# A head pair's sums moved ahead of the last score tile, its transfers moved to SyncE, and PSUM copies given precedence in the second stage

## The chip, the core and the metric

The kernel runs on one core of one Trainium2 chip. The metric is device microseconds of one execution; a median of three runs is given, and one further execution was taken with the hardware profiler. Engines are named as in the profile: PE is TensorE (PEld its weight loads), DVE is VectorE, ACT is ScalarE, POOL is GpSimd, SP is SyncE, which only issues transfers here.

## What is computed

Soft-capped attention over 4 batches of 12 heads (448 tokens, 64 dimensions each), whose output, as 1792 rows of 768, goes through a two-layer block with a rational activation:

```python
scores = cap * np.tanh(scale * np.matmul(q, k.transpose(0, 1, 3, 2)) / cap)
attn = np.exp(scores - np.max(scores, axis=-1, keepdims=True))
attn = attn / (np.sum(attn, axis=-1, keepdims=True) + 1e-09)
x = np.matmul(attn, v)            # then heads side by side: 1792 x 768
h = x @ w_in                      # 768 x 2048
P = a[0] + a[1] * h + a[2] * h2 + a[3] * h3
Q = 1.0 + np.abs(b[0]) * np.abs(h) + np.abs(b[1]) * h2
out = (P / (Q + 1e-6)) @ w_out    # 2048 x 768
```

Every product is carried at nearly full float32 precision by splitting both factors in a high and a low part and adding three products. `w_in` and `w_out` arrive as 8-byte floats and are rebuilt on the chip as 4-byte ones.

## The kernel before, in words

**Attention** walks over 24 pairs of heads, `p` = 0 to 23. Each pair has up to four score tiles (`scores`, L412: `n` = 0, 1, 2, and on odd pairs a tile 3 that holds the last 64 keys of both pairs). ACT takes the hyperbolic tangent in place in PSUM (`softmax`, L424) and the exponential into SBUF (`exp`, L442); DVE adds the exponentials of a pair's tiles up (L448, tiles `es`). `pv` (L496) multiplies with the values, `pv_tails` (L513) adds the last 64 keys. Score tiles rotate over three two-bank PSUM tiles (`ps_127`, `ps_128`, `ps_129` in the listings, `PS[0]` to `PS[2]`); the PV products use the banks `pv` and `mi`.

`norm(k)` handles the two pairs 2k and 2k+1 together. `sums` (L541) lets PE add the exponentials over keys, into `mi`, for the very last `k` into `PS[2]`. DVE copies the result out (L545). Four small transfers gather it into a compact tile (`sc`, in the listings `arena_f<-arena_f`); DVE adds a guard and takes the reciprocal (L554, L555); one transfer writes that to DRAM (`dn<-arena_f`) and two broadcast it back (`arena_r<-dn`). Each waits for the one ahead. The last `norm` has these seven transfers on SP's queue, all others on POOL's. `xout` (L574) then multiplies each pair's PV output with it, and `split_x` makes the high part on ACT (L585) and the low part on DVE (L586).

**The second stage** walks over 8 groups `g` of 256 hidden columns, two halves `m` of the tokens, and two 128-column units `y`: 32 units. `stage1` (L778) is 36 matmuls into one PSUM tile. `rational` (L809 to L822) is a chain of ACT steps (absolute value, square, linear term, logarithm L814, exponential L816, cast L821) and DVE steps (L813, L815, L817, L818, L819, L820, L822). `stage2` (L847) multiplies with `w_out`: for each pair of units 7 tiles of 128 tokens, 12 matmuls each, alternately in `PS[1]` and in the banks `pv` and `mi`. The result is copied out of PSUM: for `m` = 0 by ACT into one of three buffers (L874), from which it is written or added to `out`; for `m` = 1 into accumulators, in the first group by ACT (L877), later by DVE (L880). `make_w` rebuilds a weight tile (ACT L725, DVE L727, L730, L733) and splits it (ACT L755, DVE L757); its load (`load_w`, 768 KB, on SP) needs the one raw buffer that the steps before have read.

**What sets the order.** Every step is recorded by `self.op` with a cost, its reads and its writes, and `Plan.flush` orders them engine by engine, on modelled times: of the steps that are ready about when an engine comes free it takes the one with the lowest `prio`, which is the place in the program minus `early`. In the chip each engine and each queue then works strictly in that order. The place in the program during attention is set by `visits(p)`, a list written by hand for each pair:

```python
            return [s0, s1, (pv, p - 1), s2, t, *new, (norm, p // 2 - 1)]
```

So on an odd pair `p` the sums of the pairs `p - 3` and `p - 2` come after all four score tiles; on the last pair, 23, these are the sums of pairs 20 and 21, `norm(10)`. The sums of pairs 22 and 23, `norm(11)`, follow after attention.

Of the kernel before, what the change touches and what calls it, by code (L numbers as in the profile page):

```python
# [16 lines left out]
ALU = mybir.AluOpType  # L17
# [4 lines left out]
PE, ACT, DVE, POOL, SP = range(5)  # L22
# [5 lines left out]
def f32(ap):  # L28
    return ap.bitcast(F32)


def act_ns(n, psum, ptrs=0):
    return 0.833 * n + (110 if psum else 150) + 95 * ptrs


def dve_ns(n, ptrs=0, fast=False):
    return (0.52 if fast else 1.042) * n + 147 + 61 * ptrs
# [20 lines left out]
PV_NS = 2220  # L58
TAIL_NS = 870
D_NS = 1430  # L60


class Plan:
# [174 lines left out]
class Body:  # L238
# [284 lines left out]
    def norm(self, k):  # L523

        nc = self.nc
        end = self.last_norm(k) and self.bounded
        D, dk = (self.PS[2][:, 0, 0:448], ("ps", 2)) if end else (self.MI[:, 0:448], "mi")  # L530
        DB, sc, dn = self.DB, self.SC[k % 2], self.dn[k % 2]
        es = [self.es[(2 * k + x) % 4] for x in range(2)]
        tail, tk = self.etile(2 * k, 3)

        def sums():
            for last in range(2):
                for j in range(2):
                    for x in range(2):
                        h = 32 * (2 * j + x)
                        st, mv = (self.half[x], tail[:, j]) if last else (self.ones, es[x][:, j])  # L540
                        m = nc.tensor.matmul(D[h:h + 32], st, mv, start=not last, stop=last == 1)  # L541
            return m

        self.op(PE, D_NS + SHAPE_NS, sums, [("es", (2 * k + x) % 4) for x in range(2)] + [tk, "ones"], [dk, "turn"])
        self.op(DVE, dve_ns(448), lambda: nc.vector.tensor_copy(DB, D), [dk], ["db"], early=E_EV)  # L545
        q = SP if self.last_norm(k) else POOL
        for h in range(4):
            self.dma(q, sc[8 * h:8 * h + 8], DB[32 * h:32 * h + 1].rearrange("o (s t) -> o s t", s=8), ["db"],
                     [("sc", k % 2, h)])
        keys = [("sc", k % 2, h) for h in range(4)]  # L550
        guard = self.c["guard"][0:32] if self.bounded else 1e-9

        def small():
            nc.vector.tensor_scalar(sc, sc, guard, None, ALU.add)  # L554
            return nc.vector.reciprocal(sc, sc)  # L555

        self.op(DVE, 740, small, ["guard"], keys)
        self.dma(q, dn.rearrange("h (s t) -> (h s) t", s=8), sc, keys, [("dn", k % 2)])
        i = k % len(self.BC)
        for j in range(2):  # L560
            self.dma(q, f32(self.BC[i])[64 * j:64 * j + 64].rearrange("p x t -> p (x t)"),
                     dn[2 * j:2 * j + 2].rearrange("x t -> (x t)").unsqueeze(0).broadcast_to([64, 2 * self.S]),
                     [("dn", k % 2)], [("bc", i, x, j) for x in range(2)])
# [24 lines left out]
    def attention(self):  # L588

        nc = self.nc  # L590
        P1 = self.B * self.NP
# [22 lines left out]
        k, q, pv, tails = self.prep_k, self.prep_q, self.pv, self.pv_tails  # L614

        def visits(p):

            new = [(k, p + 2), (q, p + 2)] * (p + 2 < P1)
            s0, s1, s2, t = ((tile, p, n) for n in range(4))
            if not self.bounded:  # L620
                if p == 0:
                    return [s0, (k, 1), (q, 1), s1, s2, *new]
                if not p % 2:
                    return [s0, s1, s2, *new]
                return [s0, s1, s2, t, *new, (self.exp_shifted, p - 1), (self.exp_shifted, p), (pv, p - 1), (pv, p),
                        (tails, p), (norm, p // 2)]
            if p == 0:
                return [s0, s1, s2, (k, 1), (q, 1)]
            if p == 1:
                return [s0, s1, (k, 2), s2, t, (q, 2), (pv, 0), (k, 3), (q, 3)]  # L630
            if not p % 2:
                return [s0, s1, s2, (pv, p - 1), (tails, p - 1), *new]
            return [s0, s1, (pv, p - 1), s2, t, *new, (norm, p // 2 - 1)]

        for p in range(P1):
            m = 0
            for fn, *x in [*visits(p), (None,)]:
                if fn:
                    fn(*x)
                if fn and (fn is not tile or x[1] == 3):  # L640
                    continue
                n = x[1] if fn else 2
                if (p, m) == (0, 0):
                    self.load(1, [(self.qset(0)[0], "ql")])
                    self.load_v(1, [(self.qset(0)[0], "ql")])
                if m == 3 and p % 2 == 0:
                    self.load32(p // 2 + 1, [("scores", p, n)])
                    self.load_v(p // 2 + 1, [("scores", p, n)])
                for step in range(4 * (p % 2), 4 * (p % 2) + 4):
                    if step < 5 and step % 4 == m:  # L650
                        self.load(p // 2 + 2, [("scores", p, n)], step, 5)
                self.early_w(p, m, n)
                for kc, at in enumerate(XSPLIT):
                    if at == (p - P1, m):
                        self.split_x(0, kc)
                if todo and m == 3:
                    t = todo.pop(0)
                    if t is not None:
                        self.xout(t)
                m += 1  # L660
        if self.bounded:
            self.pv(P1 - 1)
            self.pv_tails(P1 - 1)
            norm(P1 // 2 - 1)
# [159 lines left out]
    def stage2(self, g, m, t):  # L824
# [34 lines left out]
        acc, ws = self.acc[t], self.ws  # L859
        ie = self.nev % len(self.ev)  # L860
        ev = self.ev[ie]
# [5 lines left out]
        for src, key, cs in parts:  # L867
            n = cs.stop - cs.start

            def v(t, cs=cs, src=src):  # L870
                return t[:, cs].rearrange("p (a b) -> p a b", b=384) if len(src.shape) > 2 else t[:, cs]

            if not m:
                self.op(ACT, act_ns(n, True), lambda o=v(ev), src=src: nc.scalar.mul(o, src, ws), [key],  # L874
                        [("ev", ie, cs.start)])
            elif g == 0:
                self.op(ACT, act_ns(n, True), lambda o=v(acc), src=src: nc.scalar.mul(o, src, ws), [key],  # L877
                        [("acc", t, cs.start)])
            else:
                self.op(DVE, dve_ns(n), lambda o=v(acc), src=src: nc.vector.scalar_tensor_tensor(  # L880
                    o, src, ws, o, ALU.mult, ALU.add), [key], [("acc", t, cs.start)])
        r0 = m * 2 * self.S + 128 * t
        if not m:

            ek, sums = [("ev", ie, 0), ("ev", ie, 384)], self.io["out"][r0:r0 + 128, :]
# [4 lines left out]
        elif last:  # L890
            ak = [("acc", t, 0), ("acc", t, 384)]
            for n in range(2 if end else 0):
                cs = slice(384 * n, 384 * n + 384)
# [332 lines left out]
```

## Time and profile before

| | us |
|---|---|
| median of 3 runs (678.97 to 681.29) | 679.75 |
| the profiled execution | 681.08 |
| its span in the profile | 679.2 |
| PE busy | 660.1 (97%) |
| DVE busy | 545.2 (80%) |
| ACT busy | 445.4 (66%) |
| POOL busy | 100.3 (15%) |

Attention takes the span's first 196 us, the second stage the rest. The share of busy time is a mean over stages: that PE is busy for 97% says which engine sets the time, not what a stage waits for. The idle time of PE, 19 us in all, is in pieces, and each is read from the timeline of the engines around it. A bracket such as [1.38 <-ACT etiles L821] in a timeline says how long the engine was idle before the instruction and what released it.

### The profile page before, as it was taken

How to read it: one execution, taken by the hardware profiler on the slowest of the kernel's cores; microseconds unless marked ns; L12 is line 12 of the kernel's file. 1: busy time of each engine (PE TensorE's matmuls, PEld its weight loads, DVE VectorE, ACT ScalarE, POOL GpSimd, SP SyncE). 2: the span in 40 equal slices, each digit the busy share in tenths (PEclk: the TensorE clock that was granted, in tenths of full speed). 3: DMA queues.
4: the chain of work that ended last, by engine and by line, in shares of the span. 5: the costliest groups of instructions: out<-in, count | busy, mean ns of one | idle time of the engine just before them, and what ended most of it. 6: DMA issues, size and time to landing. Idle time of an engine off the chain costs nothing.

```text
span 679.2 us, 9860 instructions
## 1 busy us (share of the span) xinstructions
PE 660.1 (97%) x3852; PEld 543.2 (80%) x3852; DVE 545.2 (80%) x677; ACT 445.4 (66%) x531; POOL 100.3 (15%) x166
## 2 busy tenths in 40 slices
PE   7999999999999899999999999999999999999996
PEld 4555555455558799999999999999989999999995
DVE  4689899989859988786977997698689869879753
ACT  5798989998947867664485557458455734864550
POOL 4023323232220000120012012001100200120030
PEclk9999999999999999999999999999999999999999
DMA  7656777663130351373177129317711931770095
GB/s 178 152 128 174 161 162 155 147 136 94 29 103 28 116 187 47 73 142 89 46 159 145 46 56 167 82 46 158 145 46 51 167 87 47 161 142 0 1 138 193
DMA packets 79879, 74.44 MB, mean 110 GB/s; under 512 B 49424, under 2 KB 68112, under 8 KB 79824
## 3 DMA queue, kind: packets, MB, share of 16 engines
q1 hardware_dynamic: 67968, 48.21, 25.3%
q0 software_dynamic: 10704, 25.27, 22.3%
q8 instruction: 32, 0.52, 0.3%
q10 hardware_dynamic: 1152, 0.25, 0.2%
q14 instruction: 23, 0.19, 0.1%
HBM read 47.98 MB, written 25.65 MB: 108 GB/s over the span
## 4 chain that ended last, share of the span: by engine, by line
issue 56%; PE 27%; ACT 6%; POOL 6%; DMA 3%; DVE 1%; ACTq 0%; POOLq 0%; DVEq 0%
PE ps L412 8%; POOL out_dram L285 6%; PE ps L778 4%; PE mi L496 4%; PE pv L496 3%; ACT ps L424 2%; ACT etiles L442 2%; PE mi L541 2%; PE pv L513 1%; PE ps L333 1%; DMA out_dram<-arena_f 1%; PE ps L356 1%; PE ps L847 1%; DMA arena_f<-in_k_dram 1%; DMA ring<-in_v_dram 1%
## 5 line engine op out<-in xcount | busy, mean ns | idle before, releaser
L778 PE MATMUL ps<-arena_r,ring 128*128 128x512 f32 (+1 forms) x1152 | 248.7, 368 | 0.5 <-ACT etiles L442 0.5
L778 PEld LDWEIGHTS ps<-arena_r,ring 128*128 128x128 f32 x1152 | 209.3, 188 | 26.6 <-ACT etiles L442 1.3
L285 POOL DMA_DIRECT2D out_dram<-arena_f x49 | 42.8, 886 | 416.6 <-ACT arena_f L874 412.6
L847 PE MATMUL ps<-arena_r,etiles 128*128 128x384 f32 x462 | 90.3, 335 | 3.0 <-ACT arena_f L874 1.5
L424 ACT ACTIVATE ps<-ps 128x896 f32<-128x896 f32 x84 | 74.4, 907 | 20.2 <-PE ps L412 19.7
L847 PEld LDWEIGHTS ps<-arena_r,etiles 128*128 128x128 f32 x462 | 81.0, 188 | 5.1 <-ACT arena_f L874 1.8
L809 ACT ACTIVATE arena_f<-ps,b 128x896 f32<-128x896 f32 x32 | 32.3, 1009 | 80.1 <-PE ps L778 80.1
L442 ACT ACTIVATE etiles<-ps,acap 128x896 f32<-128x896 f32 x84 | 82.3, 1012 | 1.0
L813 DVE SCALAR_TENSOR_TENSOR arena_f<-arena_f,bab 128x896 f32<-128x896 f32 x32 | 36.8, 1151 | 55.2 <-ACT arena_f L810 55.2
L847 PE MATMUL pv<-arena_r,etiles 128*128 128x384 f32 x231 | 77.0, 335 | 0.0
L847 PE MATMUL mi<-arena_r,etiles 128*128 128x384 f32 x231 | 76.8, 334 | 0.0
L412 PE MATMUL ps<-arena_r 64*128 64x448 f32 x576 | 72.0, 384 | 4.8 <-DVE arena_r L341 2.0
L412 PEld LDWEIGHTS ps<-arena_r 64*128 64x128 f32 x576 | 51.3, 187 | 30.1 <-ACT etiles L442 6.9
L821 ACT CAST etiles<-arena_f 128x896 fp32r<-128x896 f32 x32 | 30.1, 939 | 43.5 <-DVE arena_f L820 43.5
L818 DVE SCALAR_TENSOR_TENSOR arena_f<-arena_f,one 128x896 f32<-128x896 f32 x32 | 36.8, 1149 | 16.0 <-ACT arena_f L816 16.0
L847 PEld LDWEIGHTS pv<-arena_r,etiles 128*128 128x128 f32 x231 | 43.3, 188 | 1.2
L847 PEld LDWEIGHTS mi<-arena_r,etiles 128*128 128x128 f32 x231 | 43.3, 188 | 0.0
L847 PE MATMUL ps<-ring,etiles 128*128 128x384 f32 x210 | 42.3, 335 | 0.5 <-ACT arena_f L874 0.5
L874 ACT ACTIVATE arena_f<-ps 128x768 f32<-128x768 f32 x32 | 26.2, 818 | 22.9 <-PE ps L847 13.0
L725 ACT ACTIVATE arena_f<-arena_f 128x768 f32<-128x768 f32 x32 | 29.2, 913 | 17.2 <-DMA arena_f<-in_moe_w_in_dram 12.0
L847 PEld LDWEIGHTS ps<-ring,etiles 128*128 128x128 f32 x210 | 36.9, 188 | 1.4 <-ACT arena_f L874 0.8
L822 DVE TENSOR_TENSOR etiles<-arena_f,etiles 128x896 fp32r<-128x896 f32 x32 | 34.8, 1087 | 3.6 <-ACT etiles L821 3.0
(123 smaller groups left out, 1045.1 us busy)
## 6 DMA issues: line engine op xcount, KB each, us to landing
out_dram<-arena_f POOLq DMA_DIRECT2D x49, 384.0 KB, 6.1
arena_f<-in_moe_w_out_dram SPq DMA_DIRECT2D x16, 768.0 KB, 4.2
arena_f<-in_moe_w_in_dram SPq DMA_DIRECT2D x16, 768.0 KB, 7.4
out_dram<-arena_f SPq DMA_DIRECT2D x13, 384.0 KB, 3.4
ring<-in_q_dram SPq DMA_DIRECT2D x44, 112.0 KB, 4.0
arena_r<-dn POOLq DMA_DIRECT2D x22, 224.0 KB, 4.5
ring<-in_k_dram SPq DMA_DIRECT2D x33, 128.0 KB, 4.4
ring<-in_v_dram SPq DMA_DIRECT2D x11, 384.0 KB, 3.5
```

Of the source, the lines that this page charges most:

```text
L285: self.op(eng, (625 if local else 450) if eng == SP else 1050, lambda: e.dma_start(out, in_, **accum), r, w, nbytes=nbytes, **kw)
L412: m = nc.tensor.matmul(self.PS[i][:, j, 0:448], st[r], mv[r], start=y == 0, stop=y == len(ops) - 1)
L424: self.op(ACT, act_ns(896, True), lambda: nc.scalar.activation(ps, ps, AF.Tanh), ["table"], pk)
L442: self.op(ACT, act_ns(size, sk[0][0] == "ps", 1), lambda: nc.scalar.activation(e, src, AF.Exp, scale=acap), sk + ["table"], [ek])
L496: m = nc.tensor.matmul(po[64 * j:64 * j + 64, 0:448], raw["v"][:, 2 * x + j, 64 * c:64 * c + 64], tiles[c][0][:, j], start=c == 0, stop=False)
L778: r = nc.tensor.matmul(po[:, ts], w[:, y, kc], x, start=kc == 0 and z == 0, stop=kc == KC - 1 and z == 2)
L809: self.op(ACT, act_ns(n, True, 1), lambda: T.activation(Bt, h, AF.Abs, scale=b[:, 0:1]), hk, bk)
L813: self.op(DVE, dve_ns(n, 1), lambda: stt(Bt, C, bab[:, 1:2], Bt, ALU.mult, ALU.add), ck + ["bab"], bk)
L818: self.op(DVE, dve_ns(n, 1), lambda: stt(Bt, Bt, one, C, ALU.add, ALU.mult), ck, bk)
L821: self.op(ACT, act_ns(n, False), lambda: T.copy(GH(), A), ak, K("gh", ig) + first)
L822: self.op(DVE, dve_ns(n), lambda: V.tensor_tensor(GL(), A, f32(GH()), ALU.subtract), ak + K("gh", ig), K("gl", ig))
L847: r = nc.tensor.matmul(po[n][:, 0:384], st, mv[:, 384 * n:384 * n + 384], start=(y == 0 and x == 0), stop=(y == self.NCH - 1 and x == 2))
```

## The change

Three edits go together. On the last pair the sums of `norm(10)` are put ahead of the third score tile. The seven transfers of `norm(10)` go to SP's queue as those of `norm(11)` do. And the steps that copy the second stage's output tiles out of PSUM get `early=30`.

```diff
+E_S2 = 30
...
-        q = SP if self.last_norm(k) else POOL
+        q = SP if self.last_norm(k + 1) or self.last_norm(k) else POOL
...
-            return [s0, s1, (pv, p - 1), s2, t, *new, (norm, p // 2 - 1)]
+            sums = (norm, p // 2 - 1)
+            if p == P1 - 1:
+                return [s0, s1, (pv, p - 1), sums, s2, t]
+            return [s0, s1, (pv, p - 1), s2, t, *new, sums]
...
                 self.op(ACT, act_ns(n, True), lambda o=v(ev), src=src: nc.scalar.mul(o, src, ws), [key],
-                        [("ev", ie, cs.start)])
+                        [("ev", ie, cs.start)], early=E_S2)
             elif g == 0:
                 self.op(ACT, act_ns(n, True), lambda o=v(acc), src=src: nc.scalar.mul(o, src, ws), [key],
-                        [("acc", t, cs.start)])
+                        [("acc", t, cs.start)], early=E_S2)
             else:
                 self.op(DVE, dve_ns(n), lambda o=v(acc), src=src: nc.vector.scalar_tensor_tensor(
-                    o, src, ws, o, ALU.mult, ALU.add), [key], [("acc", t, cs.start)])
+                    o, src, ws, o, ALU.mult, ALU.add), [key], [("acc", t, cs.start)], early=E_S2)
```

What the planner makes of it is seen at three places. (Line numbers of the changed kernel are larger by 1, in the second stage by 4.)

On PE, at the last pair of heads, before (the tiles after `<-` are the factors; L412 is a score tile, L541 the sums, L778 stage one, L496 the PV product):

```order
L412 MATMUL ps_128<-arena_r 128x448 x6
L412 MATMUL ps_129<-arena_r 128x448 x6
L496 MATMUL pv<-etiles,ring_141 64x448 x6
L412 MATMUL ps_127<-arena_r 128x448 x6
L412 MATMUL ps_128<-arena_r 128x448 x12
L541 MATMUL mi<-arena_f 32x448 x4
L541 MATMUL mi<-etiles,arena_f 32x448 x4
L778 MATMUL ps_127<-arena_r,ring_1764 128x512
```

and now:

```order
L413 MATMUL ps_128<-arena_r 128x448 x6
L413 MATMUL ps_129<-arena_r 128x448 x6
L497 MATMUL pv<-etiles,ring_141 64x448 x6
L542 MATMUL mi<-arena_f 32x448 x4
L542 MATMUL mi<-etiles,arena_f 32x448 x4
L413 MATMUL ps_127<-arena_r 128x448 x6
L413 MATMUL ps_128<-arena_r 128x448 x12
L497 MATMUL mi<-etiles,ring_141 64x448 x6
```

The sums stand ahead of the tiles in `ps_127` and `ps_128`, and the last pair's PV product follows the tiles at once: six stage-one matmuls that stood between have gone behind it.

On SP, the same stretch, before (`8x1x56` are the gathers, `32x56` the reciprocals to DRAM, `64x896` the broadcasts):

```order
L285 DMA ring_141<-in_v_dram 128x4x192
L285 DMA arena_f<-in_moe_w_in_dram 128x6x256
L285 DMA arena_f<-arena_f 8x1x56 x4
L285 DMA dn<-arena_f 32x56
L285 DMA arena_r<-dn 64x896 x2
L285 DMA arena_f<-in_moe_w_out_dram 128x1536
```

and now:

```order
L286 DMA ring_141<-in_v_dram 128x4x192
L286 DMA arena_f<-arena_f 8x1x56 x4
L286 DMA arena_f<-in_moe_w_in_dram 128x6x256
L286 DMA dn<-arena_f 32x56
L286 DMA arena_r<-dn 64x896 x2
L286 DMA arena_f<-arena_f 8x1x56 x4
L286 DMA dn<-arena_f 32x56
L286 DMA arena_r<-dn 64x896 x2
L286 DMA arena_f<-in_moe_w_out_dram 128x1536
```

The seven transfers of `norm(10)` have come in; four of them stand ahead of the `w_in` load, three behind it, and those of `norm(11)` behind all of these.

On ACT, at the first output tiles of the second stage (`ps_127` holds unit 3, L874 are copies), before:

```order
L810 ACTIVATE arena_f<-ps_127 128x896
L814 ACTIVATE arena_f<-arena_f,qb 128x896
L809 ACTIVATE arena_f<-ps_127,b 128x896
L816 ACTIVATE arena_f<-arena_f,eb 128x896
L874 ACTIVATE arena_f<-ps_128 128x768
```

and now:

```order
L818 ACTIVATE arena_f<-arena_f,qb 128x896
L814 ACTIVATE arena_f<-ps_127 128x896
L820 ACTIVATE arena_f<-arena_f,eb 128x896
L878 ACTIVATE arena_f<-ps_128 128x768
L878 ACTIVATE arena_f<-pv 128x384
L878 ACTIVATE arena_f<-mi 128x384
```

One step over unit 3 (L809 before) has gone behind the copies.

On DVE, in each later group's second half of the tokens, before (L880 are copies, L813 to L822 the rational, L727 to L757 a weight tile):

```order
L813 SCALAR_TENSOR_TENSOR arena_f<-arena_f,bab 128x896
L815 TENSOR_TENSOR arena_f<-ps_129,arena_f 128x896
L880 SCALAR_TENSOR_TENSOR arena_f<-pv,arena_f 128x384
L817 SCALAR_TENSOR_TENSOR arena_f<-arena_f,a,ps_129 128x896
L818 SCALAR_TENSOR_TENSOR arena_f<-arena_f,one 128x896
L819 SCALAR_TENSOR_TENSOR arena_f<-arena_f,a 128x896
L880 SCALAR_TENSOR_TENSOR arena_f<-mi,arena_f 128x384
L820 SCALAR_TENSOR_TENSOR arena_f<-arena_f 128x896
L880 SCALAR_TENSOR_TENSOR arena_f<-ps_128,arena_f 128x768
```

and now:

```order
L817 SCALAR_TENSOR_TENSOR arena_f<-arena_f,bab 128x896
L884 SCALAR_TENSOR_TENSOR arena_f<-pv,arena_f 128x384
L884 SCALAR_TENSOR_TENSOR arena_f<-mi,arena_f 128x384
L884 SCALAR_TENSOR_TENSOR arena_f<-ps_128,arena_f 128x768
L819 TENSOR_TENSOR arena_f<-ps_129,arena_f 128x896
L822 SCALAR_TENSOR_TENSOR arena_f<-arena_f,one 128x896
...
L737 SCALAR_TENSOR_TENSOR arena_f<-arena_f 128x768
L826 TENSOR_TENSOR etiles<-arena_f,etiles 128x896
L761 SCALAR_TENSOR_TENSOR ring_2063<-arena_f,ring_2063 128x768
L884 SCALAR_TENSOR_TENSOR arena_f<-ps_128,arena_f 128x768
```

The first two tiles' copies have come ahead of L818 (L822 now); the fourth tile's copy stands at the end, behind the weight tile's steps.

## Rows read from the trace of the kernel before

**Rows 1.** Busy time by stretch: us, then PE, PEld, DVE, ACT, POOL, PEclk, DMA.

```profile
260.00:440.00 180.00, 180.00 (x954) 169.15 (x953) 143.01 (x159) 107.80 (x134) 18.54 (x21) 1.00 0.47 99
```

**Rows 2.** Timeline of PE, end of attention: start, duration, instruction, count [idle before].

```profile
185.46 2.09 PE L412 MATMUL ps<-arena_r 64*128 64x448 f32 x18
187.48 0.96 PE L541 MATMUL mi<-arena_f 128*32 128x448 f32 x8
...
189.68 1.49 PE L778 MATMUL ps<-arena_r,ring 128*128 128x512 f32 x6 [0.49 <-ACT etiles L442]
191.10 2.48 PE L496 MATMUL mi<-etiles,ring 128*64 128x448 f32 x12
...
196.06 25.05 PE L778 MATMUL ps<-arena_r,ring 128*128 128x512 f32 x120
```

**Rows 3.** Timeline of ACT, the same stretch.

```profile
186.97 1.73 ACT L424 ACTIVATE ps<-ps 128x896 f32<-128x896 f32 x2
188.60 1.93 ACT L442 ACTIVATE etiles<-ps,acap 128x896 f32<-128x896 f32 x2
```

**Rows 4.** Timeline of PE, the first output tiles.

```profile
225.52 1.39 PE L778 MATMUL ps<-arena_r,ring 128*128 128x512 f32 x6
228.29 0.96 PE L847 MATMUL ps<-arena_r,etiles 128*128 128x384 f32 x4 [1.38 <-ACT etiles L821]
...
232.57 2.38 PE L847 MATMUL ps<-arena_r,etiles 128*128 128x384 f32 x12 [1.49 <-ACT arena_f L874]
```

**Rows 5.** Timeline of DVE, from unit 0's rational to unit 1's.

```profile
204.40 1.15 DVE L813 SCALAR_TENSOR_TENSOR arena_f<-arena_f,bab 128x896 f32<-128x896 f32 x1 [1.70 <-ACT arena_f L810]
...
208.82 1.16 DVE L574 TENSOR_TENSOR arena_f<-arena_r,arena_f 128x448 f32<-128x448 f32 x2
...
210.95 2.09 DVE L586 TENSOR_TENSOR arena_r<-arena_f,arena_r 128x896 fp32r<-128x896 f32 x2
...
226.18 1.09 DVE L820 SCALAR_TENSOR_TENSOR arena_f<-arena_f 128x896 f32<-128x896 f32 x1
```

**Rows 6.** Timeline of ACT, the first output tiles.

```profile
228.15 0.91 ACT L810 ACTIVATE arena_f<-ps 128x896 f32<-128x896 f32 x1
...
230.79 1.03 ACT L816 ACTIVATE arena_f<-arena_f,eb 128x896 f32<-128x896 f32 x1
231.72 0.80 ACT L874 ACTIVATE arena_f<-ps 128x768 f32<-128x768 f32 x1
```

**Rows 7.** Timeline of PE, the one gap in the repeated part.

```profile
498.35 0.44 PE L847 MATMUL mi<-ring,etiles 128*128 128x384 f32 x1 [1.58 <-DVE arena_f L880]
```

**Rows 8.** Timeline of DVE, ahead of that gap.

```profile
495.61 1.15 DVE L818 SCALAR_TENSOR_TENSOR arena_f<-arena_f,one 128x896 f32<-128x896 f32 x1 [3.81 <-ACT arena_f L816]
```

**Rows 9.** Timeline of ACT, ahead of that gap.

```profile
492.66 0.91 ACT L725 ACTIVATE arena_f<-arena_f 128x768 f32<-128x768 f32 x1 [3.58 <-DMA arena_f<-in_moe_w_in_dram]
```

**Rows 10.** Timeline of POOL: the reciprocals of norm(10) to DRAM.

```profile
198.73 0.52 POOL L285 DMA_DIRECT2D dn<-arena_f  x1 [6.55 <-DVE arena_f L555]
```

**Rows 11.** Timeline of SP's issues, end of attention.

```profile
188.38 0.38 SPq L285 DMA_DIRECT2D arena_f<-in_moe_w_in_dram  x1
197.80 3.01 SPq L285 DMA_DIRECT2D arena_f<-arena_f  x4
```

**Rows 12.** Issues between 186 and 206: KB each, median us to landing.

```profile
arena_f<-in_moe_w_in_dram SPq DMA_DIRECT2D x1, 768.0 KB, 5.5
arena_r<-dn SPq DMA_DIRECT2D x2, 224.0 KB, 3.7
...
dn<-arena_f SPq DMA_DIRECT2D x1, 7.0 KB, 2.3
```

**Rows 13.** Issues between 88.9 and 91.2, query loads with no value load ahead.

```profile
ring<-in_q_dram SPq DMA_DIRECT2D x2, 112.0 KB, 3.6
```

**Rows 14.** Issues between 105.3 and 106.5, right behind a value load of 384 KB.

```profile
ring<-in_q_dram SPq DMA_DIRECT2D x2, 112.0 KB, 4.7
```

**Rows 15.** Issues of the whole span, the loads of w_in.

```profile
arena_f<-in_moe_w_in_dram SPq DMA_DIRECT2D x16, 768.0 KB, 7.4
```

## The prediction

> **What bounds the kernel now.** I read the windows view first. Between 260 and 440 us, deep in the second stage, TensorE's busy time is 180.00 of 180 us at full granted clock [rows 1]; VectorE and ScalarE have slack. So the time is TensorE's own work plus its idle gaps, and an edit that leaves the number of matmuls alone, as this one does, can only move gaps. I then walked TensorE's timeline for bracketed idle times. Three places with gaps lie where the change acts; the rest, at the very start and end, it does not touch.
>
> At the end of attention the sums of the tenth and eleventh head pairs (`norm(10)`) end at 189.19; TensorE idles 0.49 us, runs 6 stage-one matmuls at 189.68, the last pair's PV product from 191.10, then the tails and the last sums, and starts stage one in earnest at 196.06 [rows 2]. ScalarE works 186.97 to 190.53 on the last two score tiles [rows 3].
>
> At the start of the second stage's output products TensorE stalls in a row [rows 4]. Six stage-one matmuls begin at 225.52; at 0.21 us each (25.05 us for 120 [rows 2]) the next group should start at 226.77. The group `ps` x12 that begins at 232.57 has only 12 short matmuls ahead of it after that point, and 12 of them last 2.38 us [rows 4]. From 226.77 to 232.57 is 5.80 us, so 3.4 us are lost: the first wait is for ScalarE's cast L821 (1.38), the last for its PSUM copy L874 (1.49). What makes L821 late is VectorE, which is without a pause of note from 204.40 (unit 0's first rational step) to 227.27, the end of unit 1's L820 [rows 5]. The copy L874 started only at 231.72, when ScalarE was through with L816 [rows 6].
>
> The third gap comes once: at 498.35 TensorE has waited 1.58 us for the copy of `mi` by L880 [rows 7]. VectorE has that copy behind L818, and L818 had waited 3.81 us for ScalarE's exponential [rows 8], which stood behind L725, held 3.58 us by a weight load [rows 9]. An in-order queue turned a late load into a late PSUM copy.
>
> **The change part by part.** *Sums ahead of the third score tile.* Sums (189.19 - 187.48 = 1.7 us) and the two score tiles (185.46 to 187.48 = 2.0) change places [rows 2], so TensorE again ends both at 189.2. The third tile now ends its matmuls 0.7 us after 187.2, a third of 2.0, and its tanh can start at 188.1. Two tanh and two exponentials alternate; a pair of tanh lasts 1.73 and a pair of exponentials 1.93 [rows 3], so one of each is 0.87 + 0.97, and the third tile's exponential ends at 190.0. The PV product, which no longer has 6 stage-one matmuls ahead of it, starts then, 0.8 us after TensorE fell idle, against 0.49 before: **+0.3**. What follows PV is unchanged: 191.10 to 196.06 before, 190.0 to 195.0 now, with the 6 matmuls still owed.
>
> *Transfers on SyncE.* The sums now end at 187.2; with VectorE's copy out of PSUM, some 0.6 like a multiply of that width (1.16 for two [rows 5]), the first transfer can go at about 188.1, 1.7 us earlier. Before, the POOL transfer `dn` started at 198.73, after 6.55 us in which POOL waited for VectorE's reciprocal [rows 10]: L554 and L555, which take the landed sums, stood behind other work. Now they stand ahead of it. The cost: four issues on SyncE take 3.0 us, and the 768 KB weight load that was issued at 188.38 [rows 11] is now behind them, at about 191.1. Landing 5.5 us later [rows 12] it is there at 196.6. The steps that use it stand behind unit 0's first rational steps (204.40), so its delay costs nothing while it stays under 7 us more. `dn` follows at 193.1. Alone it lands in 2.3 us and the broadcasts in 3.7 [rows 12], so the reciprocals of `norm(10)` are in place at 199 to 200, where VectorE has idle time, rather than at its step at 208.82 [rows 5]. Behind the weight load `dn` lands later. A query load on SyncE's queue took 3.6 us [rows 13], and 4.7 right behind a 384 KB load [rows 14]. So the added delay is between nothing and 2.4 us (the weight load's landing at 196.6 plus one more, less 195.3); I take 1.1, the pair that is nearest.
>
> Four VectorE steps then leave the stretch 204 to 227: two multiplies, 1.07, and two subtractions, 2.0 [rows 5]. With 1.1 us of queue delay the rational of unit 0 starts 0.6 us later than 204.40 and its middle waits 1.1 us for the last broadcast; unit 1's L820 so ends at 227.27 - 3.07 + 0.6 + 1.1 = 225.9 at the latest, or 224.2 without the delay. TensorE, 0.3 us behind, wants the cast at about 227; a cast takes 0.9 like L810 on the same shape [rows 6], so it is there in time, if barely. The L821 wait goes.
>
> *PSUM copies take precedence.* E_S2 lets the planner put a copy up to 30 places earlier. At the first output tiles ScalarE's order becomes L814, L810, L816, L874. L810 reads unit 3's stage one, which TensorE finishes 2.1 us (12 short matmuls) before it wants the `ps` bank back. L810 (0.91), L816 (1.03) and L874 (0.80) [rows 6] with hand-overs of some 0.1 us come to 2.8: **0.7 remains** of this stall. So this place gives 3.4 - 0.7 = **-2.7**.
>
> In the repeated part the copies of `pv`, `mi` and `ps` now stand ahead of L818 on VectorE, so the 1.58 at 498 goes: **-1.6**. In exchange the fourth tile's copy stands behind the next weight tile's steps L727, L730, L733 and L757. Where a load is as late as in rows 9 I expect up to 0.6 there, otherwise nothing: **+0.3**. Among the last tiles ScalarE's order does not change, so what TensorE waits there stays.
>
> **The sum.** +0.3 - 2.7 - 1.6 + 0.3 = -3.7 on the profiled execution's 681.08 (span 679.2, and 1.9 around it): 677.4. That execution lies 0.2% over the median of the runs, 679.75; the same share off gives **676.0**.
>
> **The rivals.** *A: the queue eats the move.* If `dn` must wait for the whole weight load, both chains (`norm(10)`, then `norm(11)` behind it on SyncE) move 1.3 us beyond my value; unit 0's cast, unit 1's reads of `ps` and its subtraction then each miss TensorE by about half a us, and the first place gives 1.3 less: 677.3. For it: rows 14 against rows 13. Against it: `dn` is issued 2 us after the load, when part of that has moved. The Trainium skill (DMA: Bandwidth & Descriptors, Queues, rings and completion order) says each DMA engine consumes the descriptors of one ring in order, and SyncE has one ring on each; by that rule alone the time is this rival's 677.3, by the rows 676.0. The rows agree with the rule in sign: 1.1 us behind a load of half that size.
>
> *B: the gap moves on.* The copies come earlier, and TensorE runs into the next late thing: 2.7 us saved at 232 are lost before 262, where ScalarE carries both halves' copies. Then only the 1.6 counts, against 0.3 and 0.3: 679.75 - 1.0 = 678.7. Against it: the copies that now come first are those that TensorE waits for.
>
> *C: slower.* On ScalarE three more copies (0.80, and two of half that) stand ahead of the exponential in the group's second unit, so VectorE's weight steps, and with them the release of the single raw buffer, come some 2 us later, and every next `w_in` load starts 2 us later. TensorE comes back to the fourth tile's bank five output tiles (2.1 each) and 42 stage-one matmuls (0.21 each) after that unit's stage one, 19.3 us. From a load's landing to that copy lie eight steps over 896 columns and seven shorter, some 13 us at the 0.9 to 1.15 and about 0.5 to 0.9 of such steps [rows 5, 6]. With the issue 2 us before the unit's stage one ends, 19.3 - 13 + 2 = 8 us is the latest landing without harm; the median is 7.4 [rows 15]. There are seven groups. If loads are held as in rows 9 (3.58 beyond what ScalarE had to wait for) in most of them, at 1 to 1.5 us each, the cost is 7 to 10 us: 676 + 7 = 683. Against it: only one load in the trace was held so long.
>
> **How the numbers follow.** Forecast 0.55, A 0.17, B 0.16, C 0.12. A measurement here can tell about 0.3%, 2.0 us, from no change. Faster (below 677.7) takes nearly all of the forecast and two thirds of A: 0.66. Within: the rest of A, most of B, a little of C: 0.22. Slower: 0.12. The forecast's own range is 674.0 (no remainder of 0.7, no 0.3, the whole 1.1 absent) to 677. With A and most of B it is 673.6 to 679.4, which leaves out C and the edges, under 2 in 10.
>
> **What would show it.** Right: TensorE's first PV product of the last pair starts 0.8 us after an idle TensorE; VectorE's multiplies for pairs 20 and 21 lie before 204; no wait for L821 near 227; a wait of under 1 us for L874 near 229; none for L880 in the repeated part. A shows as those multiplies after 202 and half-us waits between 219 and 229; B as new waits for L874 or L877 between 230 and 262; C as repeated waits of `ps` for L880, 59 us apart. I am wrong if TensorE's idle sum after 200 does not fall by at least 2 us.

## The result, and the profile after

The changed kernel took 676.0 us (median of 8 executions, 673.43 to 676.26), the kernel before, beside it, 681.0 (678.97 to 682.53). The medians differ by 5.0 us; the ratio over the executions of both is 0.9912, interval 0.9897 to 0.9928: faster by 0.9%, some 6 us. Two later comparisons of the same pair gave 0.9906 (0.989 to 0.9922) and 0.9896 (0.9875 to 0.9916). The predicted time is the measured one, but by luck in part: the three executions that I set out from had a median of 679.75, the eight 681.0. I forecast a gain of 3.7 us; the ratio says 4.9 to 7.0.

The profiled execution took 673.43 us, its span 671.6. TensorE is busy for 658.4 us (98%), VectorE 546.7, ScalarE 445.7, POOL 97.0. Its waits first, from the summary by engine; before (only the lines that lie where the change acts):

```profile
PE ps L847 <- ACT arena_f L874: 1.9, 2, 1.5
PE mi L847 <- DVE arena_f L880: 1.6, 1, 1.6
...
PE ps L847 <- ACT etiles L821: 1.4, 1, 1.4
...
PE ps L778 <- ACT etiles L442: 0.5, 1, 0.5
```

and after (us in total, times, longest):

```profile
PE ps L851 <- ACT arena_f L878: 0.5, 1, 0.5
...
PE ps L851 <- DVE arena_f L821: 0.4, 1, 0.4
PE pv L514 <- ACT etiles L443: 0.3, 1, 0.3
```

Of four waits one is left, a third as long, and two small ones are new. In stretches of busy time (TensorE's is the first number behind the length of the stretch), before:

```profile
200.00:260.00 60.00, 56.97 (x293) 51.77 (x292) 52.10 (x57) 43.66 (x55) 1.04 (x2) 1.00 0.30 101
440.00:640.00 200.00, 198.42 (x1050) 185.93 (x1049) 164.42 (x187) 115.02 (x138) 18.21 (x21) 1.00 0.42 89
```

and after:

```profile
200.00:260.00 60.00, 59.09 (x304) 54.00 (x303) 54.88 (x60) 45.31 (x57) 0.00 (x0) 1.00 0.28 94
440.00:640.00 200.00, 200.00 (x1059) 187.76 (x1058) 165.90 (x186) 115.72 (x140) 18.53 (x21) 1.00 0.39 85
```

TensorE's idle time falls from 3.03 to 0.91 us in the first stretch and from 1.58 to nothing in the second. All its waits from 200 us on, summed, fall from 5.07 to 0.92 us.

At the end of attention (TensorE, answers to [rows 2]):

```profile
183.70 0.96 PE L542 MATMUL mi<-arena_f 128*32 128x448 f32 x8
...
185.34 2.11 PE L413 MATMUL ps<-arena_r 64*128 64x448 f32 x18
187.38 2.48 PE L497 MATMUL mi<-etiles,ring 128*64 128x448 f32 x12
190.10 0.59 PE L514 MATMUL pv<-etiles,ring 64*64 64x448 f32 x1 [0.25 <-ACT etiles L443]
...
192.66 25.05 PE L782 MATMUL ps<-arena_r,ring 128*128 128x512 f32 x120
```

The PV product starts without a pause at 187.38, and only the tails wait, 0.25 us. ScalarE's rows in the same stretch ([rows 3] before) tell why:

```profile
186.26 0.90 ACT L425 ACTIVATE ps<-ps 128x896 f32<-128x896 f32 x1 [0.94 <-PE ps L413]
187.20 1.01 ACT L443 ACTIVATE etiles<-ps,acap 128x896 f32<-128x896 f32 x1
188.10 0.91 ACT L425 ACTIVATE ps<-ps 128x896 f32<-128x896 f32 x1
189.04 1.01 ACT L443 ACTIVATE etiles<-ps,acap 128x896 f32<-128x896 f32 x1
```

The third tile's exponential ends at 188.21, 0.8 us after the PV product has begun: of its matmuls only the last third reads that tile.

The transfers of `norm(10)` on SP's queue ([rows 11] before), then VectorE's first rows that depend on them:

```profile
186.28 3.02 SPq L286 DMA_DIRECT2D arena_f<-arena_f  x4
189.40 0.40 SPq L286 DMA_DIRECT2D arena_f<-in_moe_w_in_dram  x1
191.27 0.35 SPq L286 DMA_DIRECT2D dn<-arena_f  x1
195.40 1.16 SPq L286 DMA_DIRECT2D arena_r<-dn  x2
```

```profile
200.01 1.16 DVE L575 TENSOR_TENSOR arena_f<-arena_r,arena_f 128x448 f32<-128x448 f32 x2 [3.96 <-DMA arena_r<-dn]
...
204.20 1.15 DVE L817 SCALAR_TENSOR_TENSOR arena_f<-arena_f,bab 128x896 f32<-128x896 f32 x1 [0.41 <-ACT arena_f L814]
...
221.99 1.08 DVE L824 SCALAR_TENSOR_TENSOR arena_f<-arena_f 128x896 f32<-128x896 f32 x1
```

The broadcasts follow `dn` 4.1 us after its issue, not 2.3 as in [rows 12]; the multiplies of pairs 20 and 21 come at 200.01, ahead of unit 0's rational, and unit 1's L824 (L820 before) ends at 223.07 instead of 227.27 [rows 5]. Of these 4.2 us, 1.77 lay there before the last pair (below); 2.4 are the chain's.

At the first output tiles, TensorE and then ScalarE ([rows 4] and [rows 6] before):

```profile
219.12 1.34 PE L851 MATMUL ps<-arena_r,etiles 128*128 128x384 f32 x6 [0.37 <-DVE arena_f L821]
...
228.05 2.35 PE L851 MATMUL ps<-arena_r,etiles 128*128 128x384 f32 x12 [0.55 <-ACT arena_f L878]
```

```profile
225.45 0.93 ACT L814 ACTIVATE arena_f<-ps 128x896 f32<-128x896 f32 x1 [0.24 <-PE ps L782]
226.27 1.03 ACT L820 ACTIVATE arena_f<-arena_f,eb 128x896 f32<-128x896 f32 x1
227.20 0.80 ACT L878 ACTIVATE arena_f<-ps 128x768 f32<-128x768 f32 x1
```

The wait for the cast L825 is gone. The wait for the copy L878 is 0.55, and its chain is what was foreseen: unit 3's stage one ends, then L814, L820, L878.

**Where the time went, by fixed points.** Four points are the same work in every kernel here: the start of pair 22's PV product (183.06 before, 181.29 after), the start of the third output tile (the `ps` x12 at 232.57 and 228.05), the end of the last copy, and the end of the span.

| us | to PV of pair 22 | to the third output tile | to the last copy's end | to the end of the span |
|---|---|---|---|---|
| before | 183.06 | 49.51 | 440.72 | 5.91 |
| after | 181.29 | 46.76 | 438.78 | 4.77 |
| after, second profile | 182.23 | 46.17 | 438.42 | 4.98 |
| after, third profile | 184.31 | 46.39 | 438.79 | 4.91 |
| sums alone | 183.84 | 48.65 | 441.96 | 5.65 |
| queue alone | 184.01 | 49.05 | 443.29 | 4.95 |
| early alone | 182.86 | 48.59 | 438.41 | 6.04 |
| sums and queue | 182.76 | 46.39 | 439.68 | 5.27 |
| sums and early | 182.67 | 48.65 | 438.52 | 5.56 |
| load behind the broadcasts | 181.04, 183.68 | 46.09, 46.10 | 438.51, 438.67 | 4.86, 4.95 |
| load on POOL | 183.16 | 47.29 | 439.47 | 4.88 |
| early on VectorE only | 183.87 | 46.59 | 439.20 | 4.84 |
| early on ScalarE only | 184.02 | 46.44 | 438.49 | 4.85 |

Nothing in the first column belongs to the change (more on it at the end): in both kernels every engine runs the same instructions in the same order up to 185 us. The other three columns give 2.75 + 1.94 + 1.14 = 5.8 us for the first profile of the changed kernel, 6.57 and 6.05 for its second and third.

### The profile page after: what moved, and what is told of

Read it like the earlier page. It is cut to its first block, busy times and chain, and to the rows that moved or that the text cites. A ratio compares the mean times of both kernels' runs of the same rounds, so it can differ in the third digit from the quotient of the medians.

```text
span 671.6 us, 9841 instructions
## 1 busy us (share of the span) xinstructions
PE 658.4 (98%) x3852; PEld 542.5 (81%) x3852; DVE 546.7 (81%) x677; ACT 445.7 (66%) x531; POOL 97.0 (14%) x159
## 4 chain that ended last, share of the span: by engine, by line
issue 57%; PE 24%; POOL 6%; ACT 5%; DMA 3%; DVE 3%; SPq 0%; ACTq 0%; POOLq 0%; DVEq 0%
PE ps L413 8%; POOL out_dram L286 6%; PE mi L497 4%; PE pv L497 3%; ACT etiles L443 2%; PE mi L542 2%; ACT ps L425 2%; PE ps L334 1%; PE pv L514 1%; DMA out_dram<-arena_f 1%; PE ps L851 1%; PE ps L357 1%; PE ps L782 1%; ACT arena_r L586 1%; DMA arena_f<-in_k_dram 1%
## 5 line engine op out<-in xcount | busy, mean ns | idle before, releaser
L825 ACT CAST etiles<-arena_f 128x896 fp32r<-128x896 f32 x32 | 30.1, 942 | 91.0 <-DVE arena_f L824 91.0
L813 ACT ACTIVATE arena_f<-ps,b 128x896 f32<-128x896 f32 x32 | 32.3, 1009 | 40.7 <-PE ps L782 40.3
L826 DVE TENSOR_TENSOR etiles<-arena_f,etiles 128x896 fp32r<-128x896 f32 x32 | 34.8, 1088 | 18.4 <-ACT etiles L825 17.6
L822 DVE SCALAR_TENSOR_TENSOR arena_f<-arena_f,one 128x896 f32<-128x896 f32 x32 | 36.7, 1148 | 16.0 <-ACT arena_f L820 15.9
L818 ACT ACTIVATE arena_f<-arena_f,qb 128x896 f32<-128x896 f32 x32 | 33.7, 1054 | 8.0 <-DVE arena_f L817 7.9
L815 ACT ACTIVATE arena_f<-ps,a 128x896 f32<-128x896 f32 x32 | 35.4, 1106 | 3.5 <-DVE arena_f L823 3.5
```

What stands on the lines that cost most here:

```text
L815: self.op(ACT, act_ns(n, True, 2), lambda: T.activation(A, h, AF.Identity, scale=a[:, 3:4], bias=a[:, 2:3]), hk, ak)
L818: self.op(ACT, act_ns(n, False, 1), lambda: T.activation(C, Bt, AF.Ln, scale=TWO_M64, bias=qb), bk + tb, ck)
L822: self.op(DVE, dve_ns(n, 1), lambda: stt(Bt, Bt, one, C, ALU.add, ALU.mult), ck, bk)
L826: self.op(DVE, dve_ns(n), lambda: V.tensor_tensor(GL(), A, f32(GH()), ALU.subtract), ak + K("gh", ig), K("gl", ig))
```

## The experiments

My theory: the first output tiles gain by the early chain of `norm(10)`, which needs the sums and the queue together; the repeated part gains by the copies' precedence. The rivals: the whole gain is one of these. The runs undo or keep parts of the change. A line that a diff does not show is as in the kernel that it names.

**One edit at a time, and two.** Against the kernel before: sums moved, queue and copies as before.

```diff
+            if p == P1 - 1:
+                return [s0, s1, (pv, p - 1), sums, s2, t]
```

> Only the sums of norm(10) are moved ahead of the third score tile; its transfers stay on POOL's queue and the PSUM copies keep their old precedence. Theory (the chain of norm(10) and the copies each give a part): the chain starts 1.8 us earlier, but VectorE's order still puts the two multiplies of pairs 20 and 21 behind unit 0's first rational step, so unit 1's cast is at most 1 us earlier: 0 to -1.5 us against before, with some of the wait for the cast L825 near 226 left, the wait for L878 near 230 left at over 1 us, and the gap for L884 near 498 left where a weight load is late. Rival (moving the sums is all that the first place needs): -2.5 us, no wait for L825.

679.09 us, ratio 0.998 (0.9966 to 0.9993). TensorE at the first output tiles, and busy time and granted clock (the last number but two) around it:

```profile
228.84 0.62 PE L851 MATMUL ps<-arena_r,etiles 128*128 128x384 f32 x2 [0.84 <-DVE etiles L826]
232.49 3.92 PE L851 MATMUL ps<-arena_r,etiles 128*128 128x384 f32 x12 [1.96 <-ACT arena_f L878]
```

```profile
228.00:232.00 4.00, 1.68 (x8) 1.36 (x8) 3.78 (x5) 4.00 (x6) 0.00 (x0) 1.00 0.50 184
232.00:236.00 4.00, 3.51 (x11) 3.51 (x12) 4.00 (x6) 2.94 (x5) 0.00 (x0) 0.57 0.50 197
```

The wait for the cast went, but part of it only moved to its successor L826 and to L878, which waits longer than before; and after that wait the granted clock fell to a mean of 0.57, so that 12 matmuls that last 2.38 in [rows 4] took 3.92. As expected in the mean, with a cost I had not expected.

Against the kernel before: the queue alone.

```diff
-        q = SP if self.last_norm(k) else POOL
+        q = SP if self.last_norm(k + 1) or self.last_norm(k) else POOL
```

> Only the seven transfers of norm(10) go to SP's queue; sums and copies as before. Theory: the sums end as late as before (189.2 on the clock of the profile of before), so the broadcasts land about 201.5 to 202.5, 1.8 us later than in the changed kernel, and VectorE's multiplies that now stand ahead of unit 0's first step wait for them; unit 1's cast comes 0.5 to 1 us earlier than before: 0 to -1 us against before. Rival (the queue is what counts): -2.5 us, as at the first output tiles of the changed kernel.

679.1 us, ratio 0.9986 (0.9966 to 1.0006): not told from no change. The same picture as the last: 0.79 for L826, 2.02 for L878, a mean clock of 0.65 in the 4 us after.

Against the kernel before: `E_S2 = 30` alone.

> Only the copies out of PSUM get early=30; sums and queue as before. Theory: the wait for the cast L825 of some 1.4 us near 227 stays, the wait for the copy L878 near 231 falls from 1.5 to about 0.5 since the exponential L820 no longer stands ahead of it, and no wait for L884 is left in the repeated part: -1.0 and, where a weight load is late, -1.6 more; -1 to -3 us against before. Rival one (the copies' precedence is the whole gain): -5 us, and both waits near 229 gone. Rival two (it is worth nothing, the chain of norm(10) is all): within 0.5 us of before.

678.12 us, ratio 0.9965 (0.995 to 0.9979). As expected:

```profile
228.10 0.96 PE L851 MATMUL ps<-arena_r,etiles 128*128 128x384 f32 x4 [1.38 <-ACT etiles L825]
...
231.45 2.35 PE L851 MATMUL ps<-arena_r,etiles 128*128 128x384 f32 x12 [0.56 <-ACT arena_f L878]
```

The cast's wait is the 1.38 of [rows 4], only the copy's has shrunk (1.49 to 0.56), and no L884 waits; the latest load held ScalarE for 2.30 us here, not the 3.58 of [rows 9].

Against the changed kernel: `E_S2 = 0`, so sums and queue without the copies' precedence.

> Sums and transfers as changed, but no early for the copies. Theory: the first output tiles look as in the changed kernel, a single wait of about 0.5 us for L878 and none for L825, since the order of ScalarE there (L818, L814, L820, L878) is the same without early; -2.5 to -3 us against before. What is left to the changed kernel (-5 us) are waits for L884 in the repeated part and the end of the kernel. Rival one (the copies' precedence is the whole gain): 0 us. Rival two (the chain of norm(10) is the whole gain): -5 us, and no wait for L884 in the repeated part.

675.54 us, ratio 0.9931 (0.9908 to 0.9954), some 4.7 us, 3.1 to 6.3. The theory's 2.5 to 3 us lie just below that, the second rival's 5 within it, so my time missed. The rows show why neither holds whole. TensorE at the first output tiles, and in the repeated part:

```profile
229.15 2.35 PE L851 MATMUL ps<-arena_r,etiles 128*128 128x384 f32 x12 [0.55 <-ACT arena_f L878]
```

```profile
553.32 0.44 PE L851 MATMUL mi<-arena_r,etiles 128*128 128x384 f32 x1 [1.13 <-DVE arena_f L884]
```

The first place is that of the changed kernel without any precedence. So ScalarE's order there, which the prediction put down to `E_S2`, comes from the early chain: with it the planner models the stretch otherwise. (With the old chain `E_S2` shortens the wait too, as the run before showed, by another order.) And a gap for L884 is back, this time in the next group; ScalarE shows the same cause as [rows 9]:

```profile
547.63 0.91 ACT L729 ACTIVATE arena_f<-arena_f 128x768 f32<-128x768 f32 x1 [3.13 <-DMA arena_f<-in_moe_w_in_dram]
```

The table of fixed points puts 3.1 us of this kernel's gain up to the third output tile, 1.0 behind it and 0.6 at the end of the span, which my expectation had left to the changed kernel.

**Second group, beside the changed kernel.**

> The changed kernel once more, as the measure for its neighbours. Theory: 675 to 676.5 us; waits as in its first profile (0.4 us for L821 near 219, 0.55 us for L878 near 228, none for L884).

674.15 us, ratio 0.9906, somewhat below what I had expected. The wait for L878 is 0.55 again; that for L821 did not show this time.

Against the changed kernel: the transfers of `norm(10)` back on POOL.

```diff
-        q = SP if self.last_norm(k + 1) or self.last_norm(k) else POOL
+        q = SP if self.last_norm(k) else POOL
```

> The changed kernel with the transfers of norm(10) back on POOL's queue. Theory (the first output tiles need the chain of norm(10) to be early, and that takes both the sums and the queue): ScalarE's order there is L818, L813, L820, L878 as with the sums alone, so the wait of some 2 us for L878 near 232 is back, with TensorE's granted clock low in the 4 us after it, as in the two runs with one of the two edits; no wait for L884. 677.5 to 679. Rival one (the copies' precedence makes up for a late chain): as the changed kernel, 676. Rival two (only a stall near 232 matters, and the low clock was chance): 2 us wait and full clock, 676.5 to 677.5.

676.75 us, ratio 0.994 (0.992 to 0.996). The first place is lost again, by 2.5 us (48.65 against 46.17 in the table), as the theory has it, but at full clock, and the time is the second rival's:

```profile
228.16 0.62 PE L851 MATMUL ps<-arena_r,etiles 128*128 128x384 f32 x2 [0.99 <-DVE etiles L826]
231.32 2.38 PE L851 MATMUL ps<-arena_r,etiles 128*128 128x384 f32 x12 [1.48 <-ACT arena_f L878]
```

The queue does matter, although the sums are early: on POOL's queue `dn` of `norm(10)` went out only at 199.15, since VectorE's reciprocals again stand behind other work. What held that work is in POOL's queue, and then on VectorE:

```profile
187.93 0.50 POOL L286 DMA_DIRECT2D arena_f<-arena_f  x1 [3.27 <-DVE arena_f L546]
188.45 1.05 POOL L286 DMA_DIRECT2D arena_r<-dn  x2
```

```profile
196.49 1.16 DVE L575 TENSOR_TENSOR arena_f<-arena_r,arena_f 128x448 f32<-128x448 f32 x2 [2.82 <-DMA arena_r<-dn]
```

The first gather of `norm(10)` now stands ahead of the broadcasts of `norm(9)`, and POOL waited 3.27 us for its data. The broadcasts so went out together with the 768 KB load (188.53) and took 6.4 us to land, for 3.7 in the kernel before; VectorE waited 2.82 us for them, and the reciprocals of `norm(10)` stand behind those multiplies. With the sums alone it is the same (2.84 us). My expectation of a low clock fell, and with it that of the time.

Against the changed kernel: the `w_in` load waits for `dn`. The second edit sends it to POOL's queue instead.

```diff
+        if (f, which) == (2, "w_in") and self.bounded:
+            after = [*after, ("dn", (self.B * self.NP // 2 - 2) % 2)]
```

```diff
-            self.dma(SP, raw.rearrange("p (k f) -> p k f", f=n),
+            self.dma(POOL if f == 2 and self.bounded else SP, raw.rearrange("p (k f) -> p k f", f=n),
```

> The changed kernel with the w_in load that stands between the first four transfers and dn of norm(10) made to wait for dn, so that it is issued behind the broadcasts of norm(10) and the first four transfers of norm(11). VectorE's and ScalarE's orders are the same. Theory (dn waits in its queue for most of the load): dn lands 2.3 us after its issue instead of 4.1, the multiplies of pairs 20 and 21 come 1 to 1.7 us earlier, VectorE's first rational step about 1 us earlier, and the waits for L821 and L878 shrink by 0.3 to 0.9 together; against it the broadcasts of norm(11) now stand behind the load and may give half of it back: -0.9 to 0 against the changed kernel. Rival (dn is slow for the traffic of the queue's neighbours or by chance): dn still takes about 4 us and nothing moves but the load.

> The changed kernel with that one w_in load issued from POOL's queue; VectorE's and ScalarE's orders are the same. The load then moves the same bytes at the same time, but not ahead of dn in SP's queue. Theory (order within one queue): dn lands in 2.3 to 2.8 us, the broadcasts about 1.5 us earlier, the waits for L821 and L878 shrink by 0.5 to 0.9 us together; 675 to 675.5. Rival (the 768 KB take the bandwidth, whichever queue they are in): dn takes about 4 us as before, and the time stays at 676.

With the load later: 672.5 us, ratio 0.9877 (0.9861 to 0.9893), the lowest of all, and 1.65 us below the changed kernel beside it where I had expected at most 0.9. SP's issues and TensorE (line numbers are 2 larger in this kernel):

```profile
191.01 0.34 SPq L286 DMA_DIRECT2D dn<-arena_f  x1
193.29 1.15 SPq L286 DMA_DIRECT2D arena_r<-dn  x2
```

```profile
227.13 2.35 PE L853 MATMUL ps<-arena_r,etiles 128*128 128x384 f32 x12 [0.55 <-ACT arena_f L880]
```

`dn` takes 2.3 us again, so the load ahead of it had cost 1.8. But TensorE's 0.55 stays, and the table gives this kernel 46.09 where the changed one has 46.17 and 46.76: the chain was no longer on the path.

With the load on POOL: 676.72 us, ratio 0.9932 (0.9918 to 0.9945), slower than the changed kernel beside it. POOL's issue, SP's issue of `dn`, and what VectorE waited for:

```profile
189.29 0.88 POOL L286 DMA_DIRECT2D arena_f<-in_moe_w_in_dram  x1 [1.70 <-DVE ring L761]
```

```profile
195.58 0.34 SPq L286 DMA_DIRECT2D dn<-arena_f  x1
```

```profile
194.79 0.24 DVE L555 TENSOR_SCALAR arena_f<-arena_f,guard 32x56 f32<-32x56 f32 x1 [3.59 <-DMA arena_f<-arena_f]
```

Neither reading held. `dn` itself is quick (it landed in 2.1 us), but the four gathers, issued from 188.15 to 191.17 while the load moved beside them on the other queue, landed only at 194.8, 3.6 us after the last issue; with the load behind them on SP (the changed kernel) it is 1.2 (189.30 to 190.48). So here a small transfer was held by a large one in either queue; what freed it was that the load came after it. That is one execution of this kernel, but the broadcasts of `norm(9)` above, on POOL's queue beside the load on SP's, agree.

**Third group.** The changed kernel, the later load again, and each half of the third edit alone (`early=E_S2` only on VectorE's line, only on ScalarE's two).

> The changed kernel, for comparison with the three beside it: 674 to 676.5 us; 0.55 us for L878 near 228, no wait for L884.

> The kernel with the w_in load behind the broadcasts of norm(10), once more beside the changed kernel. Theory (the chain of norm(10) is no longer on the path once VectorE has some spare; TensorE's 0.55 us wait for L878 hangs on unit 3's stage one and ScalarE alone): between 0 and 0.6 us less than the changed kernel, the wait for L878 unchanged at 0.55, none for L821. Rival (the 1.65 us by which it was ahead is real): 1.2 to 2 us less.

> Of the third edit only VectorE's line (L884, the second half's copies in the later groups) keeps its early=30; ScalarE's two lines have none. Theory (the third edit works through VectorE's copies alone, since ScalarE's order at the first output tiles already follows from the early chain): as the changed kernel, no wait for L884, 0.55 us for L878: 674 to 676.5. Rival (ScalarE's copies carry it): a wait for L884 of 1 us or more near 490, or new waits for L878 or L881 between 230 and 262, and 1 to 2 us above the changed kernel.

> The reverse: ScalarE's two lines keep early=30, VectorE's line has none. Theory: the late weight load near 490 again holds VectorE's copy L884 behind the rational step that waits for ScalarE's exponential, a wait of 1 to 1.6 us for L884 there, and 0.8 to 1.5 us above the changed kernel. Rival (what ScalarE does ahead of the load decides): no wait for L884, as the changed kernel.

They took 675.01, 674.74, 675.15 and 675.57 us: ratios 0.9896, 0.9892, 0.9894 and 0.9902, each within 0.0025 either way, not to be told apart. For the later load that is the theory; the lead of 1.65 us did not come back. By the time, either half of the precedence alone is not told apart from both; nor does the time show what the third edit adds to the other two (0.9931, 0.9908 to 0.9954, without it). The expectation for ScalarE's half missed: no L884 waits in its profile, though VectorE's order is the old one. The load near 490 was there in time in that execution, near 547 it held L729 for 1.30 us, and that makes no gap. All four profiles without any precedence (before, sums, queue, sums and queue) have one or two gaps for L884 of 1.1 to 1.6 us, each after a load that held ScalarE for 3 us or more (3.58, 3.34 and 3.09 near 493, 3.28 and 3.13 near 550); the ten others have none of it on `mi`.

But in eight of these ten no load held ScalarE for more than 2.30 us, so they do not test VectorE's order. Two do: the load on POOL's queue (3.67) and the precedence on VectorE only (3.25). ScalarE and TensorE in the first:

```profile
549.47 0.90 ACT L729 ACTIVATE arena_f<-arena_f 128x768 f32<-128x768 f32 x1 [3.67 <-DMA arena_f<-in_moe_w_in_dram]
```

```profile
562.75 1.32 PE L851 MATMUL ps<-arena_r,etiles 128*128 128x384 f32 x6 [0.72 <-DVE arena_f L884]
```

After the late load no copy of `mi` is late, but the fourth tile's copy, behind the weight tile's steps, costs 0.72 us, and 0.28 in the other, where I had expected no wait for L884. So in these two VectorE's precedence works as the prediction has it, at a smaller price than the 1.1 to 1.6 us without it. The loads are another matter: all five profiles without ScalarE's precedence have one that held ScalarE for over 3 us, of the nine with it only one (the load on POOL's queue). It looks as if ScalarE's earlier copies bring the loads earlier; how, no run here shows.

## Why the prediction was right, and where it was off

- **PV product behind the third tile: +0.3 foreseen, 0.2 gained.** The step that failed is that the PV product starts when the third tile's exponential ends, "0.8 us after TensorE fell idle". The product's matmuls wait one by one; the first two thirds read tiles that were ready. Idle time there went from 0.49 to 0.25.
- **The chain of `norm(10)`: right, with one term too small.** At the start of the pair-22 product, the first column of the table, the two kernels are 1.77 us apart; with that added, the first transfer goes at 188.05 (foreseen 188.1), `dn` at 193.04 (193.1), and the multiplies come at 201.8, ahead of unit 0's rational (foreseen: data in place at 199 to 200). The delay of `dn` behind the load was 1.8 us, between my 1.1 and the 2.4 of rival A: the row that I took it from has a load of half the size.
- **First output tiles: -2.7 foreseen, -2.5 measured** (2.75 less the 0.2 of the PV place; 3.1 and 2.9 in the second and third profiles). L825's wait went, L878's is 0.55 for a foreseen 0.7. A wait of 0.37 for L821 was not foreseen; the second and third profiles don't show it. One cause was named wrongly: ScalarE's order at this place comes from the early chain, not from `E_S2`, as sums and queue alone showed.
- **The gap at 498: -1.6 foreseen, -1.6 measured, in part by luck.** TensorE is busy for 200.00 of 200 us there, and the +0.3 for the fourth tile's copy was not paid. But no load in this profile held ScalarE for more than 1.54 us, so neither the gap nor its price had its cause. Where a load was late, in two other kernels with VectorE's precedence, the gap went and 0.72 and 0.28 were paid, about the 0.6 foreseen for such a load.
- **The end was mis-sized.** "What TensorE waits there stays", nothing, stood in the sum. The 0.45 us wait for L874 near 660 is not in the changed kernel's list; that is chance, for its third profile has 0.42 there, and four kernels with part of the change have none. And the stretch from the last copy to the end of the span, which the prediction said the change does not touch, is 1.1 us shorter:

```profile
672.73 0.56 DVE L880 SCALAR_TENSOR_TENSOR arena_f<-mi,arena_f 128x384 f32<-128x384 f32 x1 [0.49 <-PE mi L847]
```

```profile
666.27 0.56 DVE L884 SCALAR_TENSOR_TENSOR arena_f<-mi,arena_f 128x384 f32<-128x384 f32 x1 [0.49 <-PE mi L851]
```

From the end of this row to the end of the span (679.2 and 671.6) it is 5.91 and 4.77. These items together are the 2.1 us between -3.7 and the -5.8 of the profiles: 0.5 (PV), 0.3 (fourth tile), 0.35 (the wait near 660 and rounding), 1.1 (the end), less 0.2 at the first output tiles.

**The rivals.** A's mechanism is there: in the changed kernel `dn` landed at about 195.4, 1.2 us after the load (189.40 + 4.8 = 194.2). The Trainium skill (DMA: Bandwidth & Descriptors, Queues, rings and completion order) states that the descriptors of one ring are consumed in order; this row agrees with it. A's price is not: with the load out of the way TensorE gained 0.1 to 0.7 us up to the third output tile. And the load on POOL's queue shows that order within one queue is not the whole of it. The same section of the Trainium skill says that each DMA engine takes turns between the queues that have work for it, a packet at a time; the gathers' 3.6 us agree with that in sign only. B (the gap moves on before 262) and C (late loads, the fourth tile's copy) did not come in the changed kernel: TensorE is busy for 200.00 us of each of the stretches 240 to 440 and 440 to 640. C's wait for the fourth tile's copy exists, but came once in each of two other kernels, at 0.72 and 0.28 us, not in most groups.

## What to carry to other kernels

Two stages that meet on an in-order engine are tuned by what the first stage still owes: here two multiplies and two subtractions that came 7 us earlier, into VectorE's idle time, were worth 2.5 to 3.1 us on TensorE, and neither of the two moves that this took was worth much alone (0.9 and 0.5 us up to the third output tile). When a planner makes the order, an edit also changes decisions far from it, so attribute by runs with single edits and not by the diff. And a small transfer that a chain waits for should be issued ahead of a large load, on whichever queue that is; and where it shares an in-order queue, it should not stand, still waiting for its data, ahead of a transfer that is ready.

## What was not expected of the hardware

**A stall can cost most of its length again in clock.** After waits of 0.84 and 1.96 us (sums alone), and of 0.79 and 2.02 (queue alone), TensorE's granted clock was mostly at the lower of its two levels, 1.2 instead of 2.4 GHz (means of 0.57 and 0.65 over 4 us), and in both 12 matmuls took 3.92 us for 2.35. After 1.38, 0.17 and 1.49 (before) and after 0.99 and 1.48 (sums and early) it stayed at 1.00.

**The first 20 us differ between executions of one program.** Busy time and granted clock there, before and after:

```profile
16.00:20.00 4.00, 4.00 (x26) 2.98 (x22) 1.73 (x3) 2.85 (x5) 0.00 (x0) 0.62 0.98 213
```

```profile
16.00:20.00 4.00, 4.00 (x33) 2.76 (x32) 2.36 (x4) 3.97 (x6) 0.00 (x0) 1.00 1.01 223
```

Ten of the fourteen profiles here have 0.50 to 0.69 in that stretch, four have 1.00, and the first PV product starts at 20.75 to 22.38 or at 19.15 to 20.33. The changed kernel has both (0.50 in its third profile). It may be why two medians of the changed kernel lie 1.85 us apart, and it hides any difference of that size in one execution's time; the columns of the table behind the first are free of it.

**The end of the span follows the queue.** In the four kernels with `norm(10)` on POOL's queue the stretch after the last copy is 5.56 to 6.04 us, in the ten profiles with it on SP's 4.77 to 5.27. The transfers that are issued there are the same. The difference lies in the very last steps: POOL's last DRAIN, an instruction of the closing sequence, starts 4.5 to 5.0 us after the last copy in all fourteen, and behind it the span lasts 0.9 to 1.5 us more in the four, 0.3 in the ten. What is waited for there the records do not show, so the cause stays open.
